# First-layer weights of an expert layer loaded and converted in blocks of two pieces instead of one

## The chip, the cores and the metric

The kernel runs on one core of a Trainium2 chip. The metric is the device time of one execution in microseconds. The core has four engines that compute, each with its own queue of instructions, worked off in order: PE (TensorE, matrix products), DVE (VectorE), ACT (ScalarE) and POOL (GpSimd). A fifth, SP (SyncE), only issues DMA transfers here. Engines wait for each other by semaphores. PE writes its products to PSUM; PE's matmul and its weight load (PEld) overlap.

## The reference

The kernel computes an attention with a local window and global tokens for 8 batches and 8 heads, and then an expert layer ("maxout" of three linear maps, and an output map) on the 4608 token vectors that result. In short:

```
s_g = scale * q_g @ [k_g, k_l]^T ;  out_g = softmax(s_g) @ [v_g, v_l]
s_l = scale * q_l @ [k_g, k_l within 32 positions]^T ;  out_l = softmax(s_l) @ [v_g, v_l]
x = [out_g, out_l], heads side by side          # 4608 x 512
h = max(x @ w1, x @ w2, x @ w3)                 # 512 -> 768
out = h @ w_out                                 # 768 -> 512
```

The attention inputs are float32, the weights of the expert layer float64. Batches have 512 local and 32 global positions, heads have 64 columns.

## The kernel before

**Numbers.** The expert layer is computed at more than single-pass precision: every operand is split into a high part (a copy to the type fp32r) and a low part (the difference), and a product is made of three matmuls, high by high, high by low, low by high. The helpers `copy` (line 105), `sub` (line 98) and `times` (line 117) emit such operations. Each of them picks an engine by a planner, `least`: it keeps a running load of nanoseconds for ACT ("a"), DVE ("d"), POOL ("p") and for "x", the share that DVE and POOL need in common, adds the estimated cost of the operation for each choice, and takes the choice whose highest load is the least. `spend` books fixed work; `settle(4500)`, once per iteration, lets loads that lag behind catch up.

**Weights.** The weights come as 64-bit words that hold float64 numbers: 24 pieces of 128 x 512 (512 KB each). Pieces 0 to 17 are the first layer (six column blocks f, three maps i: piece 3f + i), 18 to 23 the second layer. `load_weight` (line 160) issues the DMA of one piece from SP into `raw[n]`. From piece 6 on the DMA also waits for the first conversion step of piece n - 5 (`marks`), which paces the loads. `convert` (line 169) turns a piece into `wt[n]`, which has the same memory as `raw[n]`, in three stages with a scratch tile `c` of 128 x 512:

1. an absolute value on ACT (line 175) and two DVE steps (lines 176 and 177),
2. two DVE steps on int32 data with two inputs each (lines 180 and 181),
3. `copy` for the high part and `sub` for the low part (lines 185 and 186; they appear in the profile under lines 113 and 115, and 103, with the tile name w).

The scratch for pieces 0 to 17 are the four halves of two tiles, `spare`, which share their memory with h4 and h5, two of the six result tiles of the first layer. Pieces 18 to 23 use two tiles of their own.

**The loop.** The main loop (line 567) goes over 128 tiles of attention, 16 per batch (128 queries of two heads each). An iteration emits the transposes of the next tile's probabilities (`trans`), the scores of the tile three ahead (`next_scores`, with its softmax on DVE and ACT), the product with the values (`pv`), the loads of queries and values, and between these, by `fill`, up to 25 matmuls of the expert layer from a generator `mm`. `weight_step` (line 192) stands near the end of an iteration: it takes every conversion in progress one stage further, begins one new piece, and loads one more piece. `WS` (line 526) tells how many times it is called in iteration i. Iterations 0 to 15 handle the first half of the queries of batch 0 and then the second half, so that the expert layer of batch 0 can begin after iteration 7, on 256 of its 512 tokens; `layer1` then takes pieces 0 to 17 in order, 12 matmuls each, twice, and `layer2` pieces 18 to 23. From iteration 16 the probabilities of a tile are moved by a DMA on SP's queue (line 351) before PE transposes them. The order in which instructions stand in an engine's queue is made from this program order by the compiler's scheduler, which also moves instructions ahead where its own estimate says that they can start.

**SP's queue** holds all loads and moves, in order. Ahead of the loop stand the loads of the first keys, queries and values and of pieces 0 to 3.

Of the kernel before, what the change touches and what calls it, by code (L numbers as in the profile page):

```python
# [10 lines left out]
F32R = mybir.dt.float32r  # L11
I32 = mybir.dt.int32
BF16 = mybir.dt.bfloat16
AF = mybir.ActivationFunctionType
ALU = mybir.AluOpType
# [32 lines left out]
SYNC = mybir.DependencyInfo(mybir.DependencyClass.Sync, mybir.DependencyReason.DATA)  # L48


def f32(ap):
    return ap.bitcast(F32)


def body(ctx, tc, kin, qin, vin, min_, win, out):
    nc = tc.nc
    act, dve, pool, pe = nc.scalar, nc.vector, nc.gpsimd, nc.tensor

    const = ctx.enter_context(tc.tile_pool(name="const", bufs=1))
    att = ctx.enter_context(tc.tile_pool(name="att", bufs=2))  # L60
    xp = ctx.enter_context(tc.tile_pool(name="xp", bufs=4))
    moe = ctx.enter_context(tc.tile_pool(name="moe", bufs=1))
# [13 lines left out]
    def width(ap):  # L76
        n = 1
        for x in ap.shape[1:]:
            n *= x
        return n  # L80

    def spend(es, ns):
        for e in es:
            load[e] += ns

    def least(costs):
        if not shared[0]:
            costs = {es[0]: ns for es, ns in costs.items()}
        es = min(costs, key=lambda es: max(load[e] for e in es) + costs[es])
        spend(es, costs[es])  # L90
        return es[0]

    def settle(ns):
        top = max(load.values()) - ns
        for e in load:
            load[e] = max(load[e], top)

    def sub(out, a, b, psum=False):
        n, k = width(out), 0 if shared[0] else 45
        c = {"d" if psum else "dx": n * 1.04 + 75 + k + (40 if k and psum else 0)}  # L100
        if not psum:
            c["px"] = n * 2.32 + 80 + k
        (dve if least(c) == "d" else pool).tensor_tensor(out=out, in0=a, in1=b, op=ALU.subtract)  # L103

    def copy(out, a, psum=False):
        n, k = width(out), 0 if shared[0] else 75
        c = {"a": n * 0.833 + (80 if psum else 110) + k}
        if psum:
            c["d"] = n * 1.04 + 80 + k
        else:  # L110
            c["dx"] = n * 0.52 + 75 + k
        if least(c) == "d":
            dve.tensor_copy(out=out, in_=a)
        else:
            act.copy(out=out, in_=a)  # L115
# [32 lines left out]
    raw, wt = {}, {}  # L148

    def weight(n, a):  # L150
        return wt[n][:, 512 * a:512 * a + 512]

    xg = const.tile([128, NP, B, SG], F32, name="xg")
    turned = psT.tile([128, 512], F32, name="T")
    dve.memset(turned, 0.0)

    spare = [moe.tile([128, 2, 512], I32, name="spare", tag=f"h{f}") for f in (4, 5)]
    loaded, marks = [0], {}

    def load_weight():  # L160
        n = loaded[0]
        if n < 24:
            loaded[0] += 1
            raw[n] = const.tile([128, 512], mybir.dt.int64, name=f"raw{n}", tag=f"w{n}")
            d = nc.sync.dma_start(out=raw[n], in_=win[n])
            if n >= 6:
                tc.add_manual_dep(d.ins, marks[n - 5], SYNC, reason="pace")

    def convert(n):
        r = raw[n].bitcast(I32).rearrange("p (n t) -> p n t", t=2)  # L170
        if n < 18:
            c = spare[n // 2 % 2 if n < 15 else 1][:, n % 2]
        else:
            c = moe.tile([128, 512], I32, name="wct", tag="o", bufs=2)
        marks[n] = act.activation(out=f32(c), in_=f32(r)[:, :, 1], func=AF.Abs).ins.name
        dve.tensor_scalar(out=f32(c), in0=f32(c), scalar1=2.0 ** -15, scalar2=HIMAX, op0=ALU.max, op1=ALU.min)
        dve.tensor_scalar(out=c, in0=c, scalar1=0x07FFFFFF, scalar2=3, op0=ALU.bitwise_and, op1=ALU.logical_shift_left)
        spend("a", 520)
        yield
        dve.scalar_tensor_tensor(out=c, in0=r[:, :, 1], scalar=-0x40000000, in1=c, op0=ALU.bitwise_and, op1=ALU.bitwise_or)  # L180
        dve.scalar_tensor_tensor(out=c, in0=r[:, :, 0], scalar=29, in1=c, op0=ALU.logical_shift_right, op1=ALU.bitwise_or)
        spend("dx", 1900)
        yield
        wt[n] = const.tile([128, 1024], F32R, name=f"w{n}", tag=f"w{n}")
        copy(weight(n, 0), f32(c))
        sub(weight(n, 1), f32(c), f32(weight(n, 0)))
        yield

    todo = iter(range(24))
    live = []  # L190

    def weight_step():
        for c in list(live):
            next(c[0])
            c[1] += 1
            if c[1] == 3:
                live.remove(c)
        n = next(todo, None)
        if n is not None:
            c = convert(n)  # L200
            next(c)
            live.append([c, 1])
        load_weight()


    NS = 4 * B * NP
# [5 lines left out]
    def load_half(i):  # L212
        h, p = divmod(i, NP)
        c0 = 256 * h
        t = att.tile([128, 320], F32, name="kh", tag="kst") if i % 3 < 2 else att.tile([128, 320], F32, name="kh", tag="kraw", bufs=1)
        nc.sync.dma_start(out=t, in_=kin[p, :, c0:c0 + 320])
        khalf[p] = (t, c0)
# [41 lines left out]
    def load_v(s, spot=0):  # L259
        if s < NS:  # L260
            if spot % 5 < 3:
                vraw[s] = att.tile([128, 4, D], F32, name="vraw", bufs=3)
            else:
                vraw[s] = att.tile([128, 4, D], F32, name="vn", tag="vs")
            nc.sync.dma_start(out=vraw[s], in_=vin[s].rearrange("p (x d) -> p x d", d=D))
# [161 lines left out]
    def x_tile():  # L427
        return xp.tile([128, 2, SL], F32R, name="xs")
# [94 lines left out]

    mm = [None]

    WS = [1, 1, 1, 1, 1, 1, 2, 1, 1, 1, 2, 1, 1, 1, 2, 1, 1, 1, 1, 1, 1, 1, 1, 1]

    def fill(n):
        if mm[0]:
            for _ in range(n):  # L530
                next(mm[0], None)
# [3 lines left out]
    def tile_at(i):  # L535
        return SEQ[i] if i < NS else NS

    def next_scores(last):
        while ahead[0] <= last:
            i = ahead[0]  # L540
            scores(tile_at(i))
            split_q(tile_at(i + 1))
            load_q(tile_at(i + 4 if i < 12 else i + 3))
            if i < 16 and i % 2 and i // 2 + 3 < 8:
                load_half(i // 2 + 3)
            ahead[0] += 1
# [8 lines left out]
    load_q(SEQ[3])  # L555
    load_v(SEQ[1], 1)
    load_weight()
    load_half(2)
    load_weight()
    next_scores(1)  # L560
    load_v(SEQ[2], 2)
    load_weight()
    next_scores(2)
    load_v(SEQ[3], 3)
    load_weight()
    trans(SEQ[0])
    for i, sl in enumerate(SEQ):
        p, t = divmod(sl, 4)
        b = p // NP
        settle(4500)  # L570
        shared[0] = i < 26
        if i % 16 == 0 and b > 1:
            fill(400)
            mm[0] = moe_local(b - 1)
        if i >= EARLY:
            transg(sl)
        trans(tile_at(i + 1))
        first = i < 32
        fill(6 if first else 4)
        next_scores(i + 3)  # L580
        if i < 16:
            if i == 7:
                clear()
            if i in (10, 12):
                load_k((i - 2) // 2)
        elif t == 3:
            split_k(p + 2)
            if p == NP:
                load_k(6)
            load_k(p + 3)  # L590
        fill(5 if first else 4)
        pv(sl)
        if EARLY <= i < 32:
            if i == EARLY:
                side = const.tile([128, 2048], F32, name="side", tag="early")
            if i % 4 == 0:
                lates = late(i // 4 - 4)
            next(lates)
        if i >= 12:
            if t <= 1 or i in (12, 13):  # L600
                glob(p + 1 if i >= 16 else 4, t if i >= 16 else i - 12)
            elif t == 2 or i == 14:
                glob_soft(p + 1 if i >= 16 else 4)
        fill(3)
        fill(7)
        split_v(tile_at(i + 2))
        if i < 12:
            load_v(tile_at(i + 4), i + 4)
        else:
            load_v(tile_at(i + 4))  # L610
        for _ in range(WS[i] if i < len(WS) else 0):
            weight_step()
        if i < 16:
            if i % 2:
                if i < 8:
                    xs.setdefault(0, []).append(x_tile())
                split_x(xr[p][:, 2 * (i // 8):2 * (i // 8) + 2, 0:128], xs[0][p], 256 * (i // 8), 256)
            if i == 7:
                mm[0] = moe_local(0)
        elif i % 16 >= 12:  # L620
            q = b * NP + i % 16 - 12
            xs.setdefault(b, []).append(x_tile())
            split_x(xr[q][:, :, 0:128], xs[b][-1], 0, SL)
# [63 lines left out]
```

## Time and profile before

The times are device microseconds. The profile is of one execution, with the time from its first to its last instruction as its span; the profiled execution's own time is the span and what lies around it.

| | us |
|---|---|
| median of three runs | 828.13 |
| lowest and highest of them | 827.27, 829.08 |
| profiled execution, own time | 831.31 |
| its span | 829.5 |
| PE busy (share of the span) | 803.7 (97%) |
| DVE busy | 616.8 (74%) |
| ACT busy | 508.5 (61%) |
| POOL busy | 459.2 (55%) |

How to read its rows: a group's row names the line, the engine, the operation, what it writes and reads, the shapes and the count; then the busy time in us and the mean ns of one, then the engine's idle time ahead of these and what ended it. A timeline's row has the start and the length in us, and in brackets the idle time before it and what ended that. A stretch's row gives the busy time of each engine within it, the clock granted to PE as a share of full speed, the share of DMA time and GB/s. "SPq" marks an issue by SP.

### The profile page before, as it was taken

To read this page: it belongs to the slowest core of one execution; us is meant where nothing else is said; L and a number is where in the kernel's file an instruction comes from. 1 tells how busy PE (TensorE), PEld (TensorE's weight loads), DVE (VectorE), ACT (ScalarE), POOL (GpSimd) and SP (SyncE) were. 2 spreads that over 40 slices of the span, in tenths; PEclk is the share of its full clock that TensorE was granted. 3 is DMA by queue.
4 is the path that set the end of the run, shared out by engine and by line. 5 is a ranking of instruction groups with operands and counts; after the bars stand their busy time and mean duration, and the time that the engine had idled before them with its cause. 6 is when DMAs were issued, how large, how long until landed. Compare 5 with 4: busy or idle time off the path is not lost.

```text
span 829.5 us, 16594 instructions
## 1 busy us (share of the span) xinstructions
PE 803.7 (97%) x4772; PEld 685.8 (83%) x4772; DVE 616.8 (74%) x2192; ACT 508.5 (61%) x1415; POOL 459.2 (55%) x624
## 2 busy tenths in 40 slices
PE   7788999999999999999999999999999999999996
PEld 5577888888888888888888888888888888888895
DVE  6999897878888888888897888888887887421121
ACT  5987786657666766667676667666676766311110
POOL 4223345756677676756676676866786665311110
PEclk9989999999999999999999999999999999999999
DMA  9856554433334433343335333443325332100101
GB/s 309 304 185 212 167 152 148 139 127 115 109 115 136 121 92 112 99 151 102 104 109 166 116 98 92 133 138 110 93 88 166 115 93 74 61 1 1 38 14 26
DMA packets 97467, 98.16 MB, mean 118 GB/s; under 512 B 19296, under 2 KB 85856, under 8 KB 97376
## 3 DMA queue, kind: packets, MB, share of 16 engines
q1 hardware_dynamic: 97232, 96.87, 37.5%
q8 instruction: 38, 0.62, 0.3%
q14 instruction: 53, 0.43, 0.2%
q10 hardware_dynamic: 144, 0.23, 0.1%
HBM read 60.39 MB, written 8.91 MB: 84 GB/s over the span
## 4 chain that ended last, share of the span: by engine, by line
PE 86%; DMA 5%; issue 3%; DVE 2%; SPq 1%; ACT 1%; POOL 1%; POOLq 0%; DVEq 0%; ACTq 0%
PE pm L441 48%; PE pm L463 17%; PE O L409 7%; PE S L339 5%; PE T L362 2%; DMA prob<-s 2%; DMA raw<-w_in 2%; PE T L363 2%; PE S L289 2%; PE S L335 1%; DMA vraw<-v_in 1%; PE S L381 1%; PE O L401 1%; POOL w L103 1%; DMA qn<-q_in 1%
## 5 line engine op out<-in xcount | busy, mean ns | idle before, releaser
L441 PE MATMUL pm<-xs,w 128*128 128x512 f32 (+1 forms) x2160 | 488.9, 367 | 1.3 <-ACT m L115 0.9
L441 PEld LDWEIGHTS pm<-xs,w 128*128 128x128 f32 x2160 | 355.9, 191 | 52.7 <-issue 4.2
L463 PE MATMUL pm<-w,h 128*128 128x512 f32 x612 | 156.4, 396 | 0.0
L103 POOL TENSOR_TENSOR h<-m,h 128x512 fp32r<-128x512 f32 (+1 forms) x59 | 70.6, 1197 | 109.8 <-ACT h L115 109.2
L463 PEld LDWEIGHTS pm<-w,h 128*128 128x128 f32 x612 | 109.4, 188 | 19.1 <-issue 0.2
L450 DVE TENSOR_TENSOR m<-pm,m 128x512 f32<-128x512 f32 (+1 forms) x120 | 72.8, 607 | 63.1 <-PE pm L441 62.3
L344 ACT ACTIVATE s<-s,nm 128x192 f32<-128x192 f32 (+1 forms) x224 | 103.3, 462 | 22.3 <-DVE nm L342 17.6
L103 POOL TENSOR_TENSOR qs<-qraw,qs 128x256 fp32r<-128x256 f32 x100 | 76.5, 765 | 69.1 <-issue 33.2
L125 POOL TENSOR_SCALAR s<-s,z 128x224 f32<-128x224 f32 (+1 forms) x194 | 84.9, 446 | 36.5 <-ACT lox L115 18.9
L342 DVE CUSTOM_DVE_ANT_0 s<-S,mask 128x192 f32<-128x192 f32 (+1 forms) x224 | 74.8, 370 | 16.3 <-PE S L339 7.7
L103 POOL TENSOR_TENSOR vs<-vraw,vs 128x256 fp32r<-128x256 f32 x102 | 75.0, 736 | 13.3 <-ACT vs L115 6.5
L103 DVE TENSOR_TENSOR pt<-T,pt 128x512 fp32r<-128x512 f32 x102 | 70.4, 690 | 15.2 <-ACT pt L115 13.8
L409 PEld LDWEIGHTS O<-pt,vs 128*128 128x128 f32 x408 | 65.9, 188 | 10.4 <-issue 2.4
L409 PE MATMUL O<-pt,vs 128*128 128x320 f32 (+1 forms) x408 | 73.1, 300 | 1.4 <-DVE pt L103 1.4
L115 ACT CAST pt<-T 128x512 fp32r<-128x512 f32 x102 | 60.3, 592 | 16.6 <-PE T L363 14.0
L339 PEld LDWEIGHTS S<-kst,qs 128*128 128x128 f32 x400 | 59.6, 190 | 8.7
L417 DVE TENSOR_TENSOR xr<-O,lox 64x160 f32<-64x160 f32 x204 | 64.3, 315 | 2.9
L103 POOL TENSOR_TENSOR kst<-kraw,kst 64x576 fp32r<-64x576 f32 x44 | 63.9, 1453 | 4.3 <-PE S L335 1.0
L115 ACT CAST h<-m 128x512 fp32r<-128x512 f32 (+1 forms) x59 | 33.2, 562 | 52.8 <-DVE m L450 52.5
L115 ACT CAST qs<-qraw 128x256 fp32r<-128x256 f32 x93 | 38.0, 409 | 44.0 <-PE S L339 31.1
L339 PE MATMUL S<-kst,qs 128*128 128x192 f32 (+1 forms) x400 | 59.5, 270 | 0.0
L347 DVE TENSOR_SCALAR z<-z 128x1 f32<-128x1 f32 x256 | 37.2, 147 | 27.3 <-ACT s L344 18.7
(123 smaller groups left out, 1183.0 us busy)
## 6 DMA issues: line engine op xcount, KB each, us to landing
vraw<-v_in SPq DMA_DIRECT2D x122, 128.0 KB, 2.3
qraw<-q_in SPq DMA_DIRECT2D x100, 128.0 KB, 2.1
prob<-s SPq DMA_DIRECT2D x56, 224.0 KB, 2.5
raw<-w_in SPq DMA_DIRECT2D x24, 512.0 KB, 4.9
prob<-s SPq DMA_DIRECT2D x56, 192.0 KB, 2.3
out_dram<-o SPq DMA_DIRECT2D x32, 256.0 KB, 2.6
kraw<-k_in SPq DMA_DIRECT2D x25, 320.0 KB, 3.1
qn<-q_in SPq DMA_DIRECT2D x29, 128.0 KB, 3.7
```

Source lines behind the costliest of these rows:

```text
L103: (dve if least(c) == "d" else pool).tensor_tensor(out=out, in0=a, in1=b, op=ALU.subtract)
L115: act.copy(out=out, in_=a)
L125: pool.tensor_scalar(out=out, in0=a, scalar1=col, scalar2=1.0, op0=ALU.mult, op1=ALU.mult)
L339: pe.matmul(ph[j][:, 0:n], lhsT=qs[sl][:, a, 128 * j:128 * j + 128], rhs=kst[p][:, j, c0:c0 + n], start=(a == 0), stop=(a == 1))
L342: dve.tensor_tensor_reduce(out=s[:, j, 0:n], in0=ph[j][:, 0:n], in1=mask[:, (1, 0, 1, 0)[t], 32 * (t == 0):32 * (t == 0) + n], scale=-0.12 ...
L344: act.activation(out=s[:, j, 0:n], in_=s[:, j, 0:n], func=AF.Exp, bias=nm[:, j:j + 1], scale=-1.0, accum_out=z[:, j:j + 1])
L347: dve.tensor_scalar(out=z[:, j:j + 1], in0=z[:, j:j + 1], scalar1=1e-9, scalar2=None, op0=ALU.add)
L409: pe.matmul(o[:, j, 0:320].rearrange("p (a q) -> p a q", a=2)[:, :, 0:n], lhsT=vs[sl][:, 2 * j + c].rearrange("p a d -> p (a d)"), rhs=pt[ ...
L417: dve.tensor_tensor(out=xr[p][64 * j:64 * j + 64, t], in0=o[0:64, j, 0:160], in1=lo[:, j], op=ALU.add)
L441: pe.matmul(ps[:, 0:n], lhsT=weight(3 * f + i, w)[:, 128 * k:128 * k + 128], rhs=xs[k][:, a, c0:c0 + n], start=(q == 0), stop=(q == 11))
L450: dve.tensor_tensor(out=m[:, 0:n], in0=ps[:, 0:n], in1=m[:, 0:n], op=ALU.max)
L463: pe.matmul(banks[t], lhsT=hh[f][:, a, 128 * t:128 * t + 128], rhs=weight(18 + f, w), start=((f, a, w) == (0, 0, 0)), stop=((f, w) == (5, 1)))
```

## The change

The 18 pieces of the first layer are handled as nine blocks of two. A block is loaded by one DMA of 1 MB into a tile of 128 x 2 x 512 int64; every conversion step works on 1024 columns at once. The six pieces of the second layer stay single; blocks and single pieces are numbered 0 to 14 together. The scratch of a block is a tile of its own in the memory of h3, h4 or h5, by the list `PLACE`. `weight_step` is called once in every iteration, and begins and loads a block or piece only in the iterations that `WS` lists. Ahead of the loop two blocks are loaded (pieces 0 to 3, as before). A DMA waits for the first conversion step of the block three before it. Piece by piece, conversion begins in iterations 0, 2, 4, 6, 7, 9, 10, 12, 14 for the blocks and 15 to 20 for the pieces 18 to 23. The planner's booked costs for a block are 427 x 2 + 98 ns on ACT and 1600 x 2 + 300 ns on DVE, where two pieces were 2 x 520 and 2 x 1900.

```diff
     def weight(n, a):
-        return wt[n][:, 512 * a:512 * a + 512]
+        if n < 18:
+            return wt[n // 2][:, n % 2, 512 * a:512 * a + 512]
+        return wt[n - 9][:, 0, 512 * a:512 * a + 512]
...
-    spare = [moe.tile([128, 2, 512], I32, name="spare", tag=f"h{f}") for f in (4, 5)]
+    PLACE = [3, 4, 5, 3, 4, 3, 5, 4, 5]
...
     def load_weight():
-        n = loaded[0]
-        if n < 24:
+        k = loaded[0]
+        if k < 15:
             loaded[0] += 1
-            raw[n] = const.tile([128, 512], mybir.dt.int64, name=f"raw{n}", tag=f"w{n}")
-            d = nc.sync.dma_start(out=raw[n], in_=win[n])
-            if n >= 6:
-                tc.add_manual_dep(d.ins, marks[n - 5], SYNC, reason="pace")
+            m = 2 if k < 9 else 1
+            raw[k] = const.tile([128, m, 512], mybir.dt.int64, name=f"raw{k}", tag=f"w{k}")
+            if m == 2:
+                d = nc.sync.dma_start(out=raw[k], in_=win[2 * k:2 * k + 2].rearrange("t p x -> p t x"))
+            else:
+                d = nc.sync.dma_start(out=raw[k][:, 0], in_=win[k + 9])
+            if k >= 3:
+                tc.add_manual_dep(d.ins, marks[k - 3], SYNC, reason="pace")
...
-        if n < 18:
-            c = spare[n // 2 % 2 if n < 15 else 1][:, n % 2]
+        if k < 9:
+            c = moe.tile([128, 2, 512], I32, name="wct", tag=f"h{PLACE[k]}")
...
-        spend("a", 520)
+        spend("a", 427 * m + 98)
...
-        spend("dx", 1900)
+        spend("dx", 1600 * m + 300)
...
-        wt[n] = const.tile([128, 1024], F32R, name=f"w{n}", tag=f"w{n}")
-        copy(weight(n, 0), f32(c))
-        sub(weight(n, 1), f32(c), f32(weight(n, 0)))
+        t = wt[k] = const.tile([128, m, 1024], F32R, name=f"w{k}", tag=f"w{k}")
+        copy(t[:, :, 0:512], f32(c))
+        sub(t[:, :, 512:1024], f32(c), f32(t)[:, :, 0:512])
...
-    WS = [1, 1, 1, 1, 1, 1, 2, 1, 1, 1, 2, 1, 1, 1, 2, 1, 1, 1, 1, 1, 1, 1, 1, 1]
+    WS = [0, 2, 4, 6, 7, 9, 10, 12, 14, 15, 16, 17, 18, 19, 20]
...
     load_weight()
     load_half(2)
-    load_weight()
     next_scores(1)
     load_v(SEQ[2], 2)
     load_weight()
     next_scores(2)
     load_v(SEQ[3], 3)
-    load_weight()
     trans(SEQ[0])
...
-        for _ in range(WS[i] if i < len(WS) else 0):
-            weight_step()
+        weight_step(i in WS)
```

The six pieces of the second layer are loaded in iterations 12, 14, 15, 16, 17 and 18; before, they were loaded in 12, 13, 14, 14, 15 and 16.

More of the change, by code (lines that the diff above doesn't have):

```diff
@@ L169, in convert @@
-    def convert(n):
-        r = raw[n].bitcast(I32).rearrange("p (n t) -> p n t", t=2)
-        if n < 18:
-            c = spare[n // 2 % 2 if n < 15 else 1][:, n % 2]
-        else:
-            c = moe.tile([128, 512], I32, name="wct", tag="o", bufs=2)
-        marks[n] = act.activation(out=f32(c), in_=f32(r)[:, :, 1], func=AF.Abs).ins.name
+            m = 2 if k < 9 else 1
[4 more added lines that the diff above has]
+                d = nc.sync.dma_start(out=raw[k][:, 0], in_=win[k + 9])
@@ new lines, in load_weight, with convert @@
+            if k >= 3:
+                tc.add_manual_dep(d.ins, marks[k - 3], SYNC, reason="pace")
+    def convert(k):
+        r = raw[k].bitcast(I32).rearrange("p j (n t) -> p j n t", t=2)
+        if k < 9:
+            c = moe.tile([128, 2, 512], I32, name="wct", tag=f"h{PLACE[k]}")
+        else:
+            c = moe.tile([128, 1, 512], I32, name="wct", tag="o", bufs=2)
+        m = 2 if k < 9 else 1
+        marks[k] = act.activation(out=f32(c), in_=f32(r)[:, :, :, 1], func=AF.Abs).ins.name
@@ L176, in convert @@
         dve.tensor_scalar(out=f32(c), in0=f32(c), scalar1=2.0 ** -15, scalar2=HIMAX, op0=ALU.max, op1=ALU.min)
         dve.tensor_scalar(out=c, in0=c, scalar1=0x07FFFFFF, scalar2=3, op0=ALU.bitwise_and, op1=ALU.logical_shift_left)
-        spend("a", 520)
+        spend("a", 427 * m + 98)
         yield
-        dve.scalar_tensor_tensor(out=c, in0=r[:, :, 1], scalar=-0x40000000, in1=c, op0=ALU.bitwise_and, op1=ALU.bitwise_or)
-        dve.scalar_tensor_tensor(out=c, in0=r[:, :, 0], scalar=29, in1=c, op0=ALU.logical_shift_right, op1=ALU.bitwise_or)
@@ L182, in convert @@
-        spend("dx", 1900)
+        dve.scalar_tensor_tensor(out=c, in0=r[:, :, :, 1], scalar=-0x40000000, in1=c, op0=ALU.bitwise_and, op1=ALU.bitwise_or)
+        dve.scalar_tensor_tensor(out=c, in0=r[:, :, :, 0], scalar=29, in1=c, op0=ALU.logical_shift_right, op1=ALU.bitwise_or)
+        spend("dx", 1600 * m + 300)
         yield
-        wt[n] = const.tile([128, 1024], F32R, name=f"w{n}", tag=f"w{n}")
-        copy(weight(n, 0), f32(c))
-        sub(weight(n, 1), f32(c), f32(weight(n, 0)))
+        t = wt[k] = const.tile([128, m, 1024], F32R, name=f"w{k}", tag=f"w{k}")
@@ L187, in convert, with weight_step @@
+        copy(t[:, :, 0:512], f32(c))
+        sub(t[:, :, 512:1024], f32(c), f32(t)[:, :, 0:512])
         yield
-    todo = iter(range(24))
+    todo = iter(range(15))
     live = []
-    def weight_step():
+    def weight_step(begin):
         for c in list(live):
@@ L197, in weight_step @@
                 live.remove(c)
-        n = next(todo, None)
-        if n is not None:
-            c = convert(n)
+        if begin:
+            c = convert(next(todo))
             next(c)
             live.append([c, 1])
-        load_weight()
+            load_weight()
     NS = 4 * B * NP
@@ L564, in body @@
     load_v(SEQ[3], 3)
-    load_weight()
     trans(SEQ[0])
```

## The prediction

> **What bounds the kernel now.** I read the page's head first, then the stretches of the span, then the waits and the timeline inside the stretches where PE is not full.
>
> ```profile
> span 829.5 us, 16594 instructions
> PE 803.7 (97%) x4772; PEld 685.8 (83%) x4772; DVE 616.8 (74%) x2192; ACT 508.5 (61%) x1415; POOL 459.2 (55%) x624
> ...
> 10.00:44.00 34.00, 26.16 (x186) 18.37 (x186) 33.26 (x120) 28.58 (x82) 11.69 (x14) 0.97 0.86 302
> 44.00:70.00 26.00, 25.60 (x182) 22.52 (x181) 24.20 (x82) 22.06 (x62) 8.11 (x8) 0.90 0.67 219
> 70.00:100.00 30.00, 27.05 (x194) 22.51 (x194) 26.84 (x96) 21.56 (x67) 8.57 (x9) 0.94 0.59 188
> 100.00:150.00 50.00, 47.29 (x413) 41.91 (x412) 41.79 (x167) 35.81 (x109) 25.34 (x30) 0.98 0.50 147
> 150.00:250.00 100.00, 100.00 (x600) 85.30 (x600) 82.02 (x294) 66.77 (x184) 68.42 (x92) 0.99 0.38 118
> ```
>
> The columns of a stretch are its length, then the busy time of PE, PEld, DVE, ACT and POOL, the granted clock, the DMA share and GB/s. Overall PE is the bound. Nothing can be won from 150 us on, where PE has no idle time, so the conversion of the weights, which is over by then, matters only through what it does to PE before. There three stages differ. In 10 to 44 us VectorE is the bound (33.26 of 34 us busy) and PE stands idle for 34.00 - 26.16 = 7.84 us. In 44 to 70 us PE is nearly full (0.40 us idle). In 70 to 100 us PE is idle for 2.95 us while DVE has some 3 us free. Since the first layer's matmuls are used as filling for whatever PE time the attention leaves, a microsecond of PE idle time removed early is a microsecond off the end.
>
> The worst stall of the first stage shows how the conversion gets in the way.
>
> ```profile
> 40.69 1.62 POOL L103 TENSOR_TENSOR w<-spare,w 128x512 fp32r<-128x512 f32 x1 [9.34 <-ACT w L115]
> ...
> 41.19 1.39 DVE L176 TENSOR_SCALAR spare<-spare 128x512 f32<-128x512 f32 x1
> ...
> 43.43 0.47 PE L362 MATMUL T<-one,early 128*128 128x128 f32 x1 [1.77 <-ACT early L123]
> ...
> 42.27:49.10 6.83, 5.67 (x24) 5.22 (x24) 6.83 (x26) 6.48 (x18) 1.31 (x2) 0.50 0.09 24
> ```
>
> A weight subtraction holds POOL from 40.69 to 42.31; the DVE operation that begins at 41.19 needs 1.39 us and ends 0.27 us after POOL does. The softmax behind it is late, PE waits 1.77 us for its transpose, and for the 6.83 us after 42.27 PE gets half its clock, worth up to 3.4 us.
>
> **The change part by part.** Nine pairs of every conversion step become one instruction each: the ACT absolute value, four DVE steps, one copy and one subtraction. The elements stay the same; one fixed part per merged pair goes.
>
> ```profile
> L180 DVE SCALAR_TENSOR_TENSOR spare<-raw,spare 128x512 int32<-128x512 int32 x18 | 16.8, 931 | 0.0
> L181 DVE SCALAR_TENSOR_TENSOR spare<-raw,spare 128x512 int32<-128x512 int32 x18 | 12.7, 703 | 0.0
> L176 DVE TENSOR_SCALAR spare<-spare 128x512 f32<-128x512 f32 x18 | 10.5, 595 | 0.0
> L177 DVE TENSOR_SCALAR spare<-spare 128x512 int32<-128x512 int32 x18 | 7.6, 426 | 0.0
> L175 ACT ACTIVATE spare<-raw 128x512 f32<-128x512 f32 x18 | 12.2, 676 | 1.0 <-POOL w L103 0.8 <-DMA raw<-w_in 0.3
> L103 POOL TENSOR_TENSOR w<-spare,w 128x512 fp32r<-128x512 f32 x9 | 12.1, 1347 | 27.1 <-ACT w L115 26.6 <-DVE w L113 0.4
> L115 ACT CAST w<-spare 128x512 fp32r<-128x512 f32 x14 | 8.6, 615 | 0.7 <-DVE spare L181 0.7
> L103 DVE TENSOR_TENSOR w<-spare,w 128x512 fp32r<-128x512 f32 x9 | 6.2, 693 | 1.8 <-ACT w L115 1.8
> L103 DVE TENSOR_TENSOR xs<-xr,xs 128x256 fp32r<-128x256 f32 x5 | 2.1, 411 | 0.0
> L115 ACT CAST xs<-xr 128x256 fp32r<-128x256 f32 x8 | 3.2, 405 | 0.1
> L113 DVE CAST w<-spare 128x512 fp32r<-128x512 f32 x4 | 1.7, 416 | 0.0
> ...
> 76.11 0.40 DVE L176 TENSOR_SCALAR wct<-wct 128x512 f32<-128x512 f32 x1
> ...
> 76.43 0.68 DVE L181 SCALAR_TENSOR_TENSOR spare<-raw,spare 128x512 int32<-128x512 int32 x1
> ...
> 77.03 0.96 DVE L176 TENSOR_SCALAR spare<-spare 128x512 f32<-128x512 f32 x1
> ```
>
> No 1024-wide operation is in the trace, so the fixed part comes from two widths of one form. DVE subtraction: 693 ns at 512 columns, 411 at 256, that is 282 ns for 256 columns, which leaves 411 - 282 = 129 ns fixed. That is the upper bound. In the three timeline rows at the end each operation starts 0.08 us before the row above it has ended (76.11 + 0.40 = 76.51 against 76.43), so part of the fixed time is hidden already: 129 - 80 = 49 ns is the lower bound. I take 80 ns, nearer to the lower one because DVE runs back to back in this stage. Of 18 copies DVE did 4 and of 18 subtractions 9, so a pair has 4 + 4/18 + 9/18 = 4.7 DVE operations, each of which loses one fixed part: 4.7 x 80 = 0.38 us a pair, 3.4 us for nine (bounds 2.1 and 5.5). ACT by the same reckoning: 615 - 2 x (615 - 405) = 195 ns fixed, some 1.8 operations a pair, at most 0.35 us a pair; ACT is not the bound (28.58 of 34 us), so I count it at nothing, and without the cover of DVE's longer queue it could add at most 3.1 us of gain. POOL's subtraction of 1347 ns becomes one of up to 2 x 1347 = 2.69 us, with the same total.
>
> What of the 3.4 us lies on the path: before 44 us DVE works on about eight pieces, four pairs: 4 x 0.38 = 1.5 us (0.9 to 2.4), all on the path, since DVE is full and PE idle there. The other 1.9 us fall into 44 to 92 us, where they can buy only PE's idle time: the 0.4 us of 44 to 70 us, and the gap before the matmul at 80.08 (0.91 us, waiting for a result that ACT copies out; rows below), in which the last pieces are being converted. I take both: 1.3 us (0 to 1.3). Sum of gains 2.8 us.
>
> **What is lost at the start.** The first load becomes 1 MB and the first conversion must wait for all of it.
>
> ```profile
> 5.48 6.40 DMA raw<-w_in
> ...
> 9.26 0.67 ACT L175 ACTIVATE spare<-raw 128x512 f32<-128x512 f32 x1 [0.25 <-DMA raw<-w_in]
> ...
> 12.16 0.67 ACT L175 ACTIVATE spare<-raw 128x512 f32<-128x512 f32 x1
> ...
> 19.13 0.51 PE L441 MATMUL pm<-xs,w 128*128 128x256 f32 x2
> ```
>
> Piece 0 was there at 9.26, piece 1 at 5.48 + 6.40 = 11.88, with a half of keys between them on the queue. At the stretch's 302 GB/s half a megabyte takes 1.7 us (estimate from that row), so the block is there between 10.6 and 11.9, 1.4 to 2.6 us later than piece 0, and ahead of piece 1. ACT stands at that instruction, behind it the exponentials and copies of the next tiles; DVE loses the two steps it did on piece 0 meanwhile, about 0.4 + 0.4 us. The first matmul of the layer, at 19.13, comes later too, but PE's whole filling before 34 us is small. I take a loss of 0.8 us, bounds 0 (the order on ACT is made so that the wait falls later) and 2.6 us.
>
> **The loads of the second layer** move: pieces 20 to 23 were issued in iterations 14, 14, 15 and 16, now in 15 to 18. On SP's queue they stand ahead of the moves of the probabilities that PE's transposes wait for.
>
> ```profile
> 82.50 0.53 SPq L165 DMA_DIRECT2D raw<-w_in  x1
> 86.06 0.33 SPq L250 DMA_DIRECT2D qn<-q_in  x1
> 86.49 0.38 SPq L165 DMA_DIRECT2D raw<-w_in  x1
> 86.96 0.64 SPq L351 DMA_DIRECT2D prob<-s  x1
> ...
> 80.08 0.62 PE L441 MATMUL pm<-xs,w 128*128 128x256 f32 x3 [0.91 <-ACT m L115]
> 82.37 0.28 PE L362 MATMUL T<-identr,prob 128*128 128x128 f32 x1 [1.67 <-DMA prob<-s]
> ...
> 91.37 0.28 PE L362 MATMUL T<-identr,prob 128*128 128x128 f32 x1
> 95.05 0.26 PE L362 MATMUL T<-identr,prob 128*128 128x128 f32 x1 [0.35 <-DMA prob<-s]
> ```
>
> The load at 86.49 stood ahead of the move at 86.96, yet the transpose at 91.37 shows no wait: PE had first-layer matmuls until then. That filling is the cover, and I cost this edit at nothing; the price without it is a rival below. The pacing waits stay one or two iterations behind their marks; queued behind them on SP are the queries, which PE had to wait for nowhere between 10 and 150 us, so these cost nothing here.
>
> **Sum.** 2.8 - 0.8 = 2.0 us less. The profiled execution took 831.31 us (span 829.5 and 1.8 around it), so 829.3 under the profiler; it lies 3.2 us above the median of the runs shown, 828.13, so in their terms 826.1 us.
>
> [...]
>
> **The rivals.**
>
> *Wider operations stand in the way (slower).* Place: 10 to 90 us, on DVE. A subtraction of two pieces on POOL holds DVE up to 2.69 us instead of 1.35, and a softmax step in DVE's queue waits behind 1.2 to 1.3 us instead of 0.69. For it: nine subtractions went to POOL, and the 43.43 row is such a case. Against it: the sum of the stands is the same, and scores run three tiles ahead. It decides once a stand is longer than the filling that PE has at that point. Price: two stands 1.35 us longer and one more half-clock stretch of 3.4 us (worth 1.7) is 4.4 us, against the gain of 2.0: 828.13 + 2.4 = 830.5 us.
>
> *Late loads delay the transposes (slower).* Two loads now fall into iterations 17 and 18. Each takes 1.7 us of the queue by the estimate above. For it: the transpose at 95.05 already waits 0.35 us for its move. Against it: the row of 91.37. If both show on PE, 3.4 us against 2.0 gained: 829.5 us.
>
> *PE hides it (no change).* The 1.5 us saved on DVE before 44 us comes back as a wait at 49 to 83 us, where PE is full at any rate, or the order of the work shifts with no net effect: 828.1 us.
>
> *The stall of 38 to 43 us goes (much faster).* If the clock is not halved after 42.27, half of 6.83 us, 3.4 us, comes on top of 2.0: 822.7 us.
>
> [...]
>
> **How the numbers follow.** The forecast (a gain of 0.6 to 4 us) gets 0.38, the much faster case 0.07, no change 0.21, the wide operations 0.20 and the late loads 0.14. What a measurement of this kernel can tell from no change is about 0.2%, 1.7 us. That gives 0.43 for faster (a few hundredths of the forecast's own chance lie within the bound), 0.23 for the same, 0.34 for slower. The likeliest case alone spans 824 to 827.5 us. For the range, the low end is the clock case less another 1.7 us for fixed parts near their upper bound, 821; the high end is the wide operations with the start at its bound of 2.6 instead of 0.8, 832.
>
> **What would show it.** Right: DVE's busy time before 100 us down by about 3.4 us; a 1024-wide L180 step of about 1.25 us; PE idle time in 10 to 44 us near 6 us. Wrong: POOL subtractions of 2.5 us and more with a stretched DVE step and a PE wait behind them; a new wait of ACT for the first block above 1.5 us; PE waits for the moved probabilities at 88 to 100 us; or a half-clock stretch at another place, which alone could turn the sign.

## The result and the profile after

| | before | after |
|---|---|---|
| median of the four timed runs of each, us | 828.61 | 836.45 |
| lowest to highest, us | 827.27 to 830.83 | 835.92 to 836.73 |
| profiled execution, us | 831.31 | 835.92 |

The change makes the kernel slower: the ratio is 1.0096, with a 95% interval of 1.0082 to 1.0110, that is 7 to 9 us. The forecast was 2 us faster. Only 4.6 us of the loss stand between the two profiled spans, because the profiled execution of before was one of its slower ones (831.31 against a median of 828.61); the sizes below are taken from the timed runs, the places from the profiles.

The page's head of the changed kernel, and its stretches (columns as before):

```profile
span 834.1 us, 16521 instructions
PE 801.5 (96%) x4772; PEld 684.2 (82%) x4772; DVE 609.5 (73%) x2147; ACT 504.2 (60%) x1394; POOL 465.8 (56%) x627
...
10.00:44.00 34.00, 25.79 (x190) 18.74 (x190) 30.97 (x101) 25.45 (x69) 14.10 (x17) 1.00 0.90 304
44.00:70.00 26.00, 20.95 (x162) 18.34 (x159) 23.13 (x60) 18.24 (x47) 7.39 (x5) 0.93 0.57 199
70.00:100.00 30.00, 24.47 (x168) 20.22 (x166) 23.20 (x82) 21.56 (x60) 13.37 (x9) 0.89 0.54 172
100.00:150.00 50.00, 48.57 (x429) 42.64 (x428) 38.77 (x157) 35.91 (x112) 20.19 (x26) 1.00 0.50 150
```

VectorE does save: 616.8 - 609.5 = 7.3 us of its busy time over the whole span, twice the 3.4 us forecast. Not all of it is the fixed part: POOL's busy time rose by 6.6 us, and how much work moved there is not broken down here. But VectorE is no longer full where it was: in 10 to 44 us its idle time is 3.03 us, where it was 0.74. PE is idle 8.21 + 5.05 = 13.26 us between 10 and 70 us; before it was 7.84 + 0.40 = 8.24. So VectorE's saved time did not shorten the work. It became waiting, and PE waits longer too.

The groups of the wide operations, in the first 100 us, and the small softmax step that follows the exponentials:

```profile
L189 DVE SCALAR_TENSOR_TENSOR wct<-raw,wct 128x1024 int32<-128x1024 int32 x9 | 11.6, 1292 | 0.0
L188 DVE SCALAR_TENSOR_TENSOR wct<-raw,wct 128x1024 int32<-128x1024 int32 x9 | 11.3, 1260 | 0.0
L185 DVE TENSOR_SCALAR wct<-wct 128x1024 int32<-128x1024 int32 x9 | 9.7, 1076 | 0.0
L184 DVE TENSOR_SCALAR wct<-wct 128x1024 f32<-128x1024 f32 x9 | 6.6, 731 | 0.0
L103 DVE TENSOR_TENSOR w<-wct,w 128x1024 fp32r<-128x1024 f32 x5 | 6.1, 1215 | 0.0
L354 DVE TENSOR_SCALAR z<-z 128x1 f32<-128x1 f32 x42 | 5.7, 143 | 6.4 <-ACT early L351 6.3
```

In the kernel before the same softmax step (line 347 there) had this row between 10 and 100 us:

```profile
L347 DVE TENSOR_SCALAR z<-z 128x1 f32<-128x1 f32 x41 | 5.7, 141 | 3.1 <-ACT s L344 2.2 <-ACT early L344 0.8
```

VectorE now stands 6.4 instead of 3.1 us until ACT has done an exponential. On ACT the absolute value takes 1.16 and the copy 1.04 us in front of it (0.68 and 0.62 before). PE in turn waits for the scaled probabilities; its waits between 10 and 70 us add up to some 13 us after and 8.5 before. The rows for the scaled probabilities and for the operands of the first layer, in total, count and longest, after and then before:

```profile
PE T L369 <- ACT early L123: 5.6, 4, 2.8
PE pm L448 <- POOL xs L103: 2.2, 3, 1.0
PE T L369 <- POOL early L125: 2.0, 3, 0.8
```

```profile
PE T L362 <- ACT early L123: 2.9, 5, 1.8
...
PE T L362 <- POOL early L125: 0.8, 1, 0.8
PE pm L441 <- DVE xs L103: 0.4, 1, 0.4
```

The longest of them, in the timeline of the changed kernel, and the clock in the stretch behind it:

```profile
52.00 2.58 POOL L103 TENSOR_TENSOR w<-wct,w 128x1024 fp32r<-128x1024 f32 x1 [7.27 <-ACT w L115]
52.25 2.61 DVE L103 TENSOR_TENSOR xs<-xr,xs 128x256 fp32r<-128x256 f32 x1
...
54.84 1.15 DVE L185 TENSOR_SCALAR wct<-wct 128x1024 int32<-128x1024 int32 x1
...
56.16 0.88 ACT L123 ACTIVATE early<-early,z 128x224 f32<-128x224 f32 x2 [2.52 <-DVE z L354]
...
56.69 0.33 PE L369 MATMUL T<-one,early 128*128 128x128 f32 x1 [2.77 <-ACT early L123]
...
57.87:61.28 3.41, 3.41 (x20) 3.08 (x20) 3.41 (x12) 3.05 (x8) 0.00 (x0) 0.50 0.00 0
```

A subtraction of 2.58 us on POOL; a VectorE operation that took 0.41 us in the kernel before takes 2.61 us; a wide conversion step of 1.15 us follows it; ACT waits 2.52 us for the softmax step behind both; PE waits 2.77 us and then has half its clock for 3.41 us. That is the chain of the first rival, link by link, with both of its parts: the hold by POOL and the wide step in VectorE's queue. The hold is read from the first two rows: the VectorE operation began 0.25 us after POOL's and ended 0.28 us after it. Another of the same form, at 77.63 us, where POOL did nothing (0.00 us busy from 76.00 to 81.10 us), took 0.41 us.

A second long wait sits where the second rival put it:

```profile
81.05 0.91 SPq L172 DMA_DIRECT2D raw<-w_in  x2
82.78 0.60 SPq L358 DMA_DIRECT2D prob<-s  x1
...
90.02 0.34 PE L369 MATMUL T<-identr,prob 128*128 128x128 f32 x1 [4.18 <-DMA prob<-s]
```

Two loads of the second layer stand directly ahead of a move of probabilities, and PE waits 4.18 us for that move. Read alone, these two places would explain the whole loss: 2.77 + 1.7 (half of 3.41) and 4.18. The first experiments took them away.

### The profile page after: what moved, and what is told of

The parts are those of the page before. It is cut to its first block, busy times and chain, and to the rows that moved or that the text cites. A ratio compares the mean times of both kernels' runs of the same rounds, so it can differ in the third digit from the quotient of the medians.

```text
span 834.1 us, 16521 instructions
## 1 busy us (share of the span) xinstructions
PE 801.5 (96%) x4772; PEld 684.2 (82%) x4772; DVE 609.5 (73%) x2147; ACT 504.2 (60%) x1394; POOL 465.8 (56%) x627
## 4 chain that ended last, share of the span: by engine, by line
PE 85%; DVE 5%; ACT 4%; DMA 3%; issue 2%; POOL 1%; SPq 0%; POOLq 0%; ACTq 0%; DVEq 0%
PE pm L448 47%; PE pm L470 16%; PE O L416 7%; PE S L346 5%; PE T L369 2%; PE T L370 2%; PE S L296 2%; PE S L342 1%; DMA prob<-s 1%; PE O L408 1%; PE S L388 1%; ACT early L351 1%; DMA vraw<-v_in 1%; ACT s L351 1%; DMA probg<-sg 1%
## 5 line engine op out<-in xcount | busy, mean ns | idle before, releaser
L125 POOL TENSOR_SCALAR s<-s,z 128x224 f32<-128x224 f32 (+1 forms) x198 | 90.5, 465 | 39.4 <-ACT lox L115 18.0
```

What stands on the lines that cost most here:

```text
L125: pool.tensor_scalar(out=out, in0=a, scalar1=col, scalar2=1.0, op0=ALU.mult, op1=ALU.mult)
```

## The experiments

They were timed in four groups, each on one chip and with 15 to 23 runs of the kernel before beside it. Brackets give the 95% interval of the ratio to these. The median of the kernel before was 828.64 to 829.55 us in the four groups, so a difference between medians of two groups is uncertain by about 1 us.

**The subtraction never on POOL.**

```diff
-        sub(t[:, :, 512:1024], f32(c), f32(t)[:, :, 0:512])
+        if k < 9:
+            spend("dx", 1024 * 1.04 + 75)
+            dve.tensor_tensor(out=t[:, :, 512:1024], in0=f32(c), in1=f32(t)[:, :, 0:512], op=ALU.subtract)
+        else:
+            sub(t[:, :, 512:1024], f32(c), f32(t)[:, :, 0:512])
```

> The changed kernel (836.5 us) with the subtraction of the nine blocks always on VectorE, never on GpSimd; nothing else differs. Theory 1 (a block's subtraction on GpSimd, 2.4 us, holds VectorE still): the waits of 2.77 us at 56.7 us and of 1.01 us at 74.5 us go, and with the first the half-clock stretch behind it (3.41 us, worth 1.7 us): 831 to 833 us. Theory 2 (the late loads of the second layer hold up the moved probabilities): no change from this, 836 to 837 us. Theory 3 (any operation of 1024 columns delays what stands behind it, on ACT and DVE too): 835 to 838 us, since DVE then has four subtractions of 1.2 us more.

Measured: 838.74 us, 1.0108 [1.0084, 1.0132]. No gain. The wait of 2.77 us is gone from its profile, and others have come; PE's waits between 10 and 70 us now begin with

```profile
PE T L373 <- POOL early L125: 4.8, 6, 1.5
PE pm L452 <- POOL xs L103: 2.3, 2, 1.2
PE T L373 <- ACT early L123: 1.7, 3, 0.7
```

So POOL's hold belongs to that one stall; the loss does not go with it.

**The second layer's loads as before.**

```diff
-            if k >= 3:
-                tc.add_manual_dep(d.ins, marks[k - 3], SYNC, reason="pace")
+            if k >= 3:
+                tc.add_manual_dep(d.ins, marks[k - 3 if k < 9 else PACE[k - 9]], SYNC, reason="pace")
...
+    PACE = [6, 7, 7, 8, 8, 9]
+    LOADS = [0, 2, 4, 6, 7, 9, 10, 12, 13, 14, 14, 15, 16]
...
         weight_step(i in WS)
+        for _ in range(LOADS.count(i)):
+            load_weight()
```

(`weight_step` itself loads nothing then.)

> The changed kernel with the six pieces of the second layer loaded in iterations 12, 13, 14, 14, 15 and 16, as in the kernel before, paced by the block that holds the piece five before. Theory 2: the move issued at 82.78 us lands in about 2.5 instead of 7.1 us, the wait of 4.18 us before the transpose falls to 1.7 us or less and the half-clock stretch of 6.83 us behind it to 3.41 us, together some 4 us: 832 to 833 us. Theories 1 and 3: no change from this, 836 to 837 us.

Measured: 842.19 us, 1.0161 [1.0138, 1.0184]: 5.7 us slower than the change. Its profile still has waits for moved probabilities (3.6 us between 70 and 160 us, the longest 2.5) and new ones elsewhere.

**Both edits.**

> Both edits: the subtraction of the blocks on VectorE, and the loads of the second layer as before. If theories 1 and 2 both hold and add up: 826 to 829 us, at or below the kernel before (828.6 us). If only one holds: 831 to 833 us. Theory 3: 834 us and more.

Measured: 837.99 us, 1.0104 [1.0083, 1.0125]. Both rivals' places are gone or smaller (the longest wait for moved probabilities between 70 and 160 us is 0.9 us), and the loss is still whole.

**All steps 512 wide.**

```diff
-        marks[k] = act.activation(out=f32(c), in_=f32(r)[:, :, :, 1], func=AF.Abs).ins.name
+        for j in range(m):
+            marks[k] = act.activation(out=f32(c)[:, j], in_=f32(r)[:, j, :, 1], func=AF.Abs).ins.name
```

and in the same way the four VectorE steps, the copy and the subtraction; bookings 520 and 1900 ns a piece.

> The changed kernel with its loads of 1 MB, its scratch tiles and its order of blocks, but every conversion step done in two operations of 512 columns, one piece after the other, booked at the planner's former costs. Theory 3: it takes back all that width costs, and leaves the late loads: 831 to 833 us. Theory 1: the same, since GpSimd's subtraction is 1.3 us again. Theory 2: no gain, and the fixed parts come back: 837 to 840 us.

Measured: 832.54 us, 1.0035 [1.0016, 1.0054]: 4 us of the loss of 8 come back, with loads, scratch and order of the blocks as in the change. The planner's bookings came back with the width; the runs with other bookings, below, bear on that. PE's busy time between 10 and 70 us, in this kernel and then in the changed one:

```profile
10.00:70.00 60.00, 52.50 (x362) 40.14 (x362) 56.98 (x196) 48.61 (x137) 23.04 (x23) 0.94 0.79 268
```

```profile
10.00:70.00 60.00, 46.74 (x346) 37.08 (x345) 54.10 (x160) 43.69 (x116) 21.48 (x21) 0.97 0.76 258
```

With narrow steps PE is busy 52.50 of 60 us and VectorE 56.98; with wide ones 46.74 and 54.10. Some of PE's difference is its clock, 0.94 against 0.97: in instructions it is 362 against 346.

**Only ACT narrow** (absolute value and copy), then **only VectorE narrow** (four steps and subtraction), each with the edit above for these lines alone and the former booking of that engine.

> The changed kernel (836.5 us), with only the absolute value and the copy of a block done in two operations of 512 columns; the four VectorE steps and the subtraction stay 1024 wide. All narrow gave 832.5 us. If the width on ACT is what costs (1.16 and 1.04 us there in front of the exponentials): 832 to 834 us. If it is the width on VectorE: 836 to 838 us. If both together, about half: 834 to 835 us.

> The changed kernel, with only the four VectorE steps and the subtraction of a block done in two operations of 512 columns; the absolute value and the copy stay 1024 wide. If the width on VectorE is what costs (1.21 us in front of the score reductions and the small softmax steps): 832 to 834 us. If it is the width on ACT: 836 to 838 us.

Measured: 834.29 us, 1.0065 [1.0043, 1.0087], and 836.08 us, 1.0087 [1.0066, 1.0108]. Neither alone brings back what both together do.

**All narrow, and two loads of 512 KB a block.**

```diff
-                d = nc.sync.dma_start(out=raw[k], in_=win[2 * k:2 * k + 2].rearrange("t p x -> p t x"))
+                ds = [nc.sync.dma_start(out=raw[k][:, j], in_=win[2 * k + j]) for j in range(2)]
```

> All conversion steps 512 wide as in the run that gave 832.5 us, and each block loaded by two DMAs of 512 KB one behind the other instead of one of 1 MB. If the rest of the loss (3 us) comes from a first conversion that waits for a whole megabyte: 829 to 830.5 us, since the first absolute value can start when the first half has landed. If it comes from the order in which blocks are begun or from the late loads of the second layer: 832 to 833 us.

Measured: 831.18 us, 1.0028 [1.0011, 1.0045]. Between the two expectations; the next runs bear on it.

**The kernel before, with late loads of the second layer only.**

```diff
+        if loaded[0] < 18:
+            load_weight()
...
+        if i in (12, 14, 15, 16, 17, 18):
+            load_weight()
```

> The kernel before (829 us) with one part of the change alone: the six pieces of the second layer are loaded in iterations 12, 14, 15, 16, 17 and 18. If late loads in front of the moved probabilities cost by themselves (one wait of 4.2 us and a longer half-clock stretch in the changed kernel's profile): 832 to 834 us. If they only fill a gap that is there anyway: 828.5 to 830 us.

Measured: 829.45 us, 1.0004 [0.9989, 1.0020]. This part of the change costs nothing that shows by itself.

**The kernel before, with pieces begun in pairs.** The body of `weight_step` from the choice of the next piece on runs m times, with

```diff
-    WS = [1, 1, 1, 1, 1, 1, 2, 1, 1, 1, 2, 1, 1, 1, 2, 1, 1, 1, 1, 1, 1, 1, 1, 1]
+    WS = [2, 0, 2, 0, 2, 0, 2, 2, 0, 2, 2, 0, 2, 0, 2, 1, 1, 1, 1, 1, 1]
```

> The kernel before (829 us), with 512-wide steps, single loads and its own scratch, in which only the order changes: two pieces begin together in iterations 0, 2, 4, 6, 7, 9, 10, 12 and 14, as the blocks do, and one each in 15 to 20; the loads go with the beginnings. If beginning in pairs is what is left of the loss when all steps are narrow and the loads are single (831 us): 830.5 to 832 us. If what is left comes from the scratch tiles or the loads: 828 to 829.5 us.

Measured: 831.55 us, 1.0036 [1.0023, 1.0049]. This fits the first expectation, but the next run shows that it needs no cause in the pairs.

**The kernel before, with other bookings only.**

```diff
-        spend("a", 520)
+        spend("a", 476)
...
-        spend("dx", 1900)
+        spend("dx", 1750)
```

> The kernel before with nothing but the planner's booked costs changed to what the change books per piece (476 instead of 520 ns on ACT, 1750 instead of 1900 ns on VectorE): the same work, another choice of engines and another order here and there. It shows what a change of order alone is worth. If this kernel's time hangs on the exact order: 1 to 4 us either way. If not: 828 to 829.5 us.

Measured: 832.55 us, 1.0041 [1.0026, 1.0057]. The same work, the same loads, the same widths; only the choice of engines and the order differ, and it costs 2 to 5 us. So the loss of about 3 us of the kernels with narrow steps needs no cause of its own in pairs, scratch or loads: two numbers in the planner do as much. Where it goes I cannot show: the profile of this kernel is of its second fastest execution (830.56 us).

**Scratch spread over h0 to h5**, with wide steps, then with narrow steps and two loads.

```diff
-    PLACE = [3, 4, 5, 3, 4, 3, 5, 4, 5]
+    PLACE = [0, 1, 2, 3, 4, 5, 3, 4, 5]
```

> The changed kernel (836.5 us) with the blocks' scratch in the memory of h0, h1, h2, h3, h4, h5, h3, h4, h5 in turn, so that no absolute value waits for the subtraction of a block begun shortly before. In the changed kernel's profile ACT stands 2.8 us at the absolute values, with the exponentials behind it. If that wait is what width on ACT costs: 832.5 to 834.5 us. If it is the length of the operations: 836 to 837 us.

> All steps 512 wide, two loads of 512 KB a block (831 us), and the scratch spread over h0 to h5. If scratch is what is left of the loss: 828.5 to 829.5 us. If the order in pairs is: 830.5 to 832 us.

Measured: 840.22 us, 1.0139 [1.0123, 1.0155], and 831.95 us, 1.0044 [1.0030, 1.0059]. ACT's waits for scratch are gone, as the row of the wide absolute values in the first of the two shows (no idle time before them), and the kernel is slower by 4 us:

```profile
L183 ACT ACTIVATE wct<-raw 128x1024 f32<-128x1024 f32 x9 | 10.4, 1155 | 0.0
```

**The two by two again, in another order**: two loads a block, with all wide, ACT narrow, VectorE narrow.

> The changed kernel (836.5 us), all steps 1024 wide, each block loaded by two DMAs of 512 KB. If width costs 4 to 5 us whatever the order, against 831.2 us for the same loads with all steps narrow: 835 to 837 us. If the loss was one of the order alone: 830 to 833 us.

> Two loads a block; absolute value and copy 512 wide, VectorE's steps and the subtraction 1024 wide. If width on ACT is what costs: 831 to 833 us. If width on VectorE is: 835 to 837 us. If each costs half: 833 to 835 us, as the run with one load (834.3).

> Two loads a block; VectorE's steps and the subtraction 512 wide, absolute value and copy 1024 wide. If width on VectorE is what costs: 831 to 833 us. If width on ACT is: 835 to 837 us, as the run with one load (836.1). If each costs half: 833 to 835 us.

Measured, with the runs of above:

| steps | one load of 1 MB | two loads of 512 KB |
|---|---|---|
| all 1024 wide | 836.45 | 835.61 [1.0052, 1.0101] |
| ACT 512, VectorE 1024 | 834.29 | 835.76 [1.0057, 1.0108] |
| ACT 1024, VectorE 512 | 836.08 | 835.94 [1.0059, 1.0122] |
| all 512 | 832.54 | 831.18 |

Both engines wide cost 4.2 us on average against both narrow (3.9 and 4.4). With one engine wide, three of the four kernels carry nearly that whole cost; the fourth (VectorE wide, one load) carries 1.8 us of 3.9. So the two do not add up. What one load instead of two does is not to be told from nothing (0.8, -1.5, 0.1 and 1.4 us).

**The kernel before, with the subtraction never on POOL.**

```diff
-        sub(weight(n, 1), f32(c), f32(weight(n, 0)))
+        spend("dx", 512 * 1.04 + 75)
+        dve.tensor_tensor(out=weight(n, 1), in0=f32(c), in1=f32(weight(n, 0)), op=ALU.subtract)
```

> The kernel before (829 us) with the subtraction of the weight pieces always on VectorE, 0.69 us there instead of 1.35 us on GpSimd. If the holds are worth removing (its stall of 1.77 us at 43.4 us and the half-clock stretch of 6.83 us behind it follow one): 825 to 828 us. If the new order costs what the other new orders cost: 830 to 833 us.

Measured: 830.87 us, 1.0024 [1.0006, 1.0041]. Removing the holds behind its worst stall brings nothing here either.

Taken together: the seven other kernels with all steps 512 wide lie between 829.45 and 832.55 us, on average 831.4; the ten with 1024-wide steps on ACT, on VectorE or on both, the change among them, lie between 834.29 and 842.19, and the two sets do not overlap. The kernel before, at 828.1 to 829.6 us, is at the fast end of the first set. No version beats it. (These are medians; single executions of the two sets do overlap.)

The profiles put the loss before 160 us. Between 10 and 160 us PE works off 1045 to 1061 instructions in the eight kernels with all steps 512 wide, the kernel before among them with 1047, and 969 to 1042 in the ten others, the change with 1024; the total is 4772 in every one. From 160 to 700 us PE is busy 537 to 540 of 540 us in all of them.

What the runs do not separate is the width from its booking: each engine's booking was changed whenever its width was. The one kernel with the change's low bookings and narrow steps, 832.55 us, lies in the first set, which speaks against the bookings alone; but it is a variant of the kernel before, and wide steps with the former bookings were not run.

## Why the prediction was wrong

**The fixed part was right for a single operation.** It was put at 80 ns a merged operation on VectorE, with bounds of 49 and 129. Median durations, of the tile's operations, before:

```profile
L176 DVE TENSOR_SCALAR spare<-spare x18: 402/421/1394, 11.1 to 81.5; 128x512 f32<-128x512 f32 x18
...
L180 DVE SCALAR_TENSOR_TENSOR spare<-raw,spare x18: 673/692/1770, 13.1 to 84.1; 128x512 int32<-128x512 int32 x18
L181 DVE SCALAR_TENSOR_TENSOR spare<-raw,spare x18: 671/678/1102, 15.2 to 86.1; 128x512 int32<-128x512 int32 x18
```

and after (a few 512-wide ones of the second layer are among them):

```profile
L184 DVE TENSOR_SCALAR wct<-wct x12: 409/674/1081, 14.0 to 98.0; 128x1024 f32<-128x1024 f32 x9, 128x512 f32<-128x512 f32 x3
...
L188 DVE SCALAR_TENSOR_TENSOR wct<-raw,wct x11: 685/1214/1630, 16.4 to 93.8; 128x1024 int32<-128x1024 int32 x9, 128x512 int32<-128x512 int32 x2
L189 DVE SCALAR_TENSOR_TENSOR wct<-raw,wct x11: 673/1216/1710, 18.0 to 96.2; 128x1024 int32<-128x1024 int32 x9, 128x512 int32<-128x512 int32 x2
```

2 x 692 - 1214 = 170, 2 x 678 - 1216 = 140 and 2 x 421 - 674 = 168 ns by duration; less the overlap of 80 ns with the next, which the prediction read from its rows, 60 to 90 ns. The durations alone lie above the bound of 129 ns. The estimate of "about 1.25 us" for such a step was right as well.

**The step that failed** is "all on the path, since DVE is full and PE idle there", and with it the term that took PE's idle time of 44 to 100 us as further gain. VectorE did not stay full when its work was made less: its idle time in 10 to 44 us rose from 0.74 to 3.03 us. PE's idle time there should have fallen to about 6 us and was 8.21. In 44 to 70 us it should have fallen from 0.40 us to nothing and rose to 5.05; in 70 to 100 us it rose from 2.95 to 5.53. Nothing of the gain of 2.8 us can be seen.

A reading of why, which is argued and not shown: short steps of the conversion filled the spaces between the small steps of the softmax. The softmax goes VectorE, ACT, VectorE, ACT or POOL, PE, so every link can stand behind one conversion step, as it does in the rows from 52.00 us on. With steps twice as long the links wait longer, and VectorE goes idle in the meantime. VectorE's wait for the exponentials between 10 and 70 us bears this out where VectorE's own steps are wide: 4.3 to 7.5 us in these eight kernels, against 0.4 to 3.1 us in the eight with all steps narrow. It does not explain the two kernels in which only ACT's steps are wide. There that wait is 1.9 and 1.2 us and VectorE is as busy as in the kernel before (57.05 and 57.83 of 60 us, against 57.46), and they are as slow as the change all the same (836.08 and 835.94 us). PE waits 2.0 us for weight subtractions on POOL in both, which it did not in the kernel before, but no run tests that. The cause on ACT's side stays open.

**The rival of the wide operations** named the right side, and a part of its mechanism, softmax steps that stand behind wide ones in VectorE's queue, agrees with the waits. It was given 0.20. That its price of 4.4 us is near the measured 4.2 is luck: the price counts two holds by POOL, each 1.35 us longer, and one half-clock stretch of 3.4 us, and without any subtraction of a block on POOL the change is no faster; width on ACT was not in it at all. Its time of 830.5 us was too low because it still counted the gain and left out the next point. That a hold doubles with the width was the author's estimate: the VectorE operation at 41.19 us before took 1.39 us against a median of 0.42, the one at 52.25 us after 2.61 against 0.41, which makes the hold 1.2 us longer. The length of 3.4 us is that of two more stretches at half clock in the profile before, where the prediction showed only the one of 6.83 us:

```profile
83.23:86.65 3.42, 3.42 (x18) 2.92 (x18) 2.65 (x5) 2.21 (x7) 1.34 (x1) 0.50 0.48 154
...
148.09:151.50 3.41, 3.41 (x21) 3.41 (x19) 2.56 (x9) 1.63 (x4) 1.37 (x4) 0.50 0.92 255
```

**What no step had**: another order of the same work can cost this kernel about 3 us. The three runs that change nothing but the order and the choice of engines cost 0.3 us (late loads), 3.0 us (pairs) and 3.4 us (bookings); the seven changed kernels with all steps narrow cost 2.5 us on average, each against the runs beside it. The prediction took the order for neutral. The loss of 8 us can be read as some 3 us of this and the 4 to 5 us that go with the width; that the two add up so is not shown.

**The start** was forecast as a loss of 0.8 us. The first absolute value came 3.2 us later, and so did the first matmul of the layer, which stood at 19.13 before:

```profile
12.48 1.13 ACT L183 ACTIVATE wct<-raw 128x1024 f32<-128x1024 f32 x1
...
22.36 0.73 PE L448 MATMUL pm<-xs,w 128*128 128x256 f32 x4 [0.35 <-ACT w L115]
```

What this costs is not settled. Of the pairs with one load and with two, only those whose absolute value is 512 wide bring the first one forward, from 12.41 to 9.51 us with all steps narrow and from 12.34 to 10.38 with ACT narrow; the times went 1.4 us down and 1.5 us up. That does not contradict a small term.

**The late loads** were costed at nothing, and that was right as far as the run on the kernel before shows: they cost 0.3 us there by the ratio, within the interval of no change. In the change itself, loading early made the kernel slower and not faster, so the wait of 4.18 us in its profile is not shown to be what the time depends on.

## What to carry to other kernels

Merging two operations saved 0.14 to 0.17 us by duration here, but on an engine that serves a chain through several queues the length of the longest operation may count as well: cost the time that the chain's steps stand behind it, on each engine that the chain crosses, before booking the saved busy time as gain. A full engine is not proof that its saved time comes through; look whether the engine stays full (VectorE's idle time in 10 to 44 us rose from 0.74 to 3.03 us). Where a scheduler orders the queues, first time a kernel in which only the order differs: an effect smaller than that cannot be put down to the edit, and a long wait found in one profile is a cause only when a run without it is faster. Change one thing at a time for this: here the planner's bookings went with the width, and the two were never taken apart.

## What the runs showed of the hardware

Merging two steps of 512 columns into one of 1024 saved 0.14 to 0.17 us by duration on VectorE (2 x 678 - 1216 = 140 and 2 x 692 - 1214 = 170 ns). The kernels with steps of 1024 columns were about 4 us slower all the same.

Single executions of the kernel before spread from 827.17 to 833.02 us (23 runs beside one set of experiments), and with them goes the mean clock granted to PE: the eight at or below 828.1 us had 0.994 to 0.996, the four above 831.4 us 0.989 to 0.991. A half-clock stretch of 3.41 us, as in the profile above, lowers the mean of 829 us by 0.002 and is worth up to 1.7 us, so two or three more of them would make the difference by this estimate. That the clock is the cause, and does not merely fall where PE is idle longer, is not shown.
